# Attention and MLP in one kernel: first loads on two queues, warming products, a later weight pair, new step strings for two units, and half of q's turn behind a sum

## The chip, the cores and the metric

The kernel runs on one core of a Trainium2 chip. Times are device microseconds (us) of one execution, from start to end. Five engines have instruction streams of their own: PE (matrix products), DVE (vector), ACT (scalar functions and copies), POOL and SP, which in this kernel issues most of the DMAs; ACT issues a few. Lower is better.

## The reference, cut to what matters

```
for t in range(S):                                   # S = 768, per batch (4) and head (8), D = 48
    state = f[t][:, None] * state + outer(k[t], v[t])    # f = sigmoid(f_logit)
    y[t] = q[t] @ state
x = y, laid out as (4*768 tokens, 8*48 = 384)
h = x @ w_in                                         # w_in 384 x 2048
g = h * sigmoid(1.702 * h)
out = g @ w_out                                      # w_out 2048 x 384
```

## The kernel before, in words

**Tiling.** The 3072 tokens are cut into 12 units of 256. A unit goes through attention and then through the MLP. Attention works in chunks of 64 tokens with six levels (1, 2, 4, ... 32): at each level PE computes scores `sc` (L445), DVE multiplies the queries and keys by the running decay (L539 in units 0 and 1, L543 later), ACT copies keys aside (`Kc`, L514; later units also queries, `Qc`, L520) and masked scores go into a tile `A` (DVE L486 and L505; level 32 by ACT, L495). Then PE adds `A` times v into `y` (L555), forms the chunk sums `pd` (L666) from turned keys `kn` (L619, later units L641), DVE chains the states `st` (L691, L692), and PE adds query times state into `y` (L713). ACT copies `y` to `yT` (L728) and five or six DMAs lay it out as `xT` (L778, L783), the input of the MLP. For unit 0 ACT first reads one element of the finished sum (L677), so that PE's L713 stands behind L555.

**Turning the inputs.** f, q and k arrive in a tile `raw`. In units 0 and 1 PE turns them by a product with the identity (`t`, L376) and ACT moves the result out (L381). From unit 2 on DVE turns them by 32x32 transposes, two instructions for each input (L364), and POOL and ACT finish f (L391, L394).

**Weights.** They come as 64-bit numbers, in 16 pairs of row blocks, numbered 0 to 15 here: 576 KB for a pair of w_in, 768 KB for one of w_out. A pair is fetched on SP (L207) into one of three `bits` buffers, and turned into float32 by one ACT instruction (L239, the Prelu) and three of DVE (`a` L235, `s` L228, the sum L238). The fetch of a pair waits until the pair three before it has been read out of its buffer.

**MLP.** Units 0 and 1 use plain products (h L1127, gelu on ACT L1131, o L1141, running sum L1191 and L1193). Unit 3 and later use 20 products of quarter blocks for h (L1033), whose results DVE adds up (L1061) and ACT turns to g (L1052, L1063), and 7 products for o (L894).

**What sets the order.** PE's and POOL's order is that of the program text. In the opening and in units 1 and 2 ACT, DVE and SP follow the text too. The text of the opening is written out by hand (from L1311 on). After it, unit 1 and unit 2 of attention are emitted part by part, and after each part a string of steps (PLAN, L1363) says what is put in: `f` is the next MLP step (three h products or one o product), `c` the next step of converting a weight pair, `p` starts the conversion of the next pair (its ACT instruction), `w` fetches the next pair, `s` does a prepared sum of weights, `k` is an idle product that keeps the array at work. HOLES (L263) puts such steps inside unit 2's levels, and FIRST (L1362) ahead of unit 1. From unit 4 on a planner (`merge`, L1254) places MLP steps by their columns. In the opening `keep_up` (L110) issues idle products on `A`, which is cleared by a DVE memset (L121), ahead of the first loads.

**The places that the change touches.** `load_raw` (L269) deals a unit's four head pairs over the queues that it is given; the first pair of q in unit 0 takes three DMAs, because it begins one token early. The opening calls `load_raw` for f on SP alone, for k on SP, for q on ACT alone, then fetches weight pair 0 (L1316 to L1319). Late in the opening it starts weight pair 1 (L1351), ahead of the level-32 copies L495. In unit 1's strings the fetch of pair 8 stands ahead of y and xT of unit 1, and that of pair 9 behind them, next to the `p` of pair 8 (the part "pw").

Of the kernel before, what the change touches and what calls it, by code (L numbers as in the profile page):

```python
# [16 lines left out]
def view(t, offset, dims):  # L17

    a = t[:]
    return bass.AP(a.tensor, a.offset + offset, [list(a.ap[0])] + [list(d) for d in dims])  # L20
# [3 lines left out]
def kernel(  # L24
# [33 lines left out]
    nc = tc.nc  # L58
# [51 lines left out]
    def keep_up(times, columns=(NL - 1) * 64, of=None):  # L110

        if times:
            pt = bank([P, columns], f"idle_{next(serial)}")
        for _ in range(times):
            lhs, rhs = of or (ident, masks.rearrange("p l f t -> p (l f t)"))
            nc.tensor.matmul(pt, lhsT=lhs, rhs=rhs, start=True, stop=True)

    ones = const.tile([P, 1], F32, name="ones")
    nc.vector.memset(ones, 1.0)
    nc.scalar.activation(ones, ones, AF.Sigmoid)  # L120
    nc.vector.memset(A, 0.0)  # L121
    nc.vector.memset(ones, 1.0)
    serial = count()
    flat_A = A.rearrange("p c f t -> p (c f t)")
    keep_up(2, 192, (flat_A[:, :P], flat_A[:, :192]))

    R = U // 32
    RW = R * D + HS - D
# [131 lines left out]
            state["done"] += 2  # L260


    HOLES = {(N_FILL, 0): "ccp", (N_FILL, 1): "cwcc", (N_FILL, 2): "cwp", (N_FILL, 3): "cc", (N_FILL, 4): "cw"}  # L263

    def convert_in(n, l):

# [71 lines left out]
    def attention(n):  # L338
# [19 lines left out]
        def turn(j, outs, fn=None, pieces=None):  # L358

            if n >= N_FILL:  # L360
                for f in (1, 0):
                    out = outs(f)
                    at, step = (0, 1) if f else (HALF - 1, -1)
                    nc.vector.transpose(  # L364
                        view(out, at, [[HALF, NP], [step, R4], [R4 * step, 32]]),
                        by_half[:, j, f].rearrange("p a (j d) -> p (a j) d", j=R4)[:, :, :32],
                    )
                if fn:
                    fn()
                return  # L370
            for j0 in pieces or range(0, R, 4):
                pt = bank([P, 4, P], f"t_{n}_{j}_{j0}")
                for jj in range(4):
                    for h in range(2):
                        x = (j0 + jj) * D
                        nc.tensor.matmul(  # L376
                            pt[h * HS:(h + 1) * HS, jj, :], lhsT=by_pair[j][:, h, x:x + HS], rhs=ident, start=True, stop=True
                        )
                for f in (1, 0):
                    at, step = (j0, 1) if f else (HALF - 1 - j0, -1)  # L380
                    nc.scalar.activation(  # L381
                        view(outs(f), at, [[HALF, NP], [R * step, 16], [step, 4]]),
                        pt.rearrange("p j (a f i) -> p f a i j", a=NP, f=2)[:, 1 - f],
                        (AF.Tanh if n > 1 else AF.Sigmoid) if fn else AF.Copy, scale=0.5 if fn and n > 1 else 1.0,
                    )
            if fn and n > 1:
                half_up()
# [612 lines left out]
    def mlp_h20(n, g, before):  # L1000
        w = (width(n) + 1) // 2
        groups = 1 if FG * w <= 512 else 2
        wide = FG // groups
        order = WHOLE if groups == 1 else HALVES
        plan = [x for x in order if x[0] is not None]
        lane_of = {(x, group): lane for x, group, lane in plan}
        left = {}
        for x, group, _ in plan:
            for out, _ in PRODUCTS[x][3]:
                left[out, group] = left.get((out, group), 0) + 1  # L1010
        single = {key for key, times in left.items() if times == 1}
        begun, banks, shared, later = set(), {}, {}, {}
        in_y[n] = len(plan)

        def take(lane, name):
            if lane < 4:
                banks[lane] = bank([P, wide, w], f"h_{n}_{name}", lanes["h"][lane])
            else:
                tag = "y" if lane < 6 else "sc"
                if tag not in shared:  # L1020
                    shared[tag] = ps.tile([P, 2, 512], F32, tag=tag, name=f"h_{n}_{tag}")
                banks[lane] = shared[tag][:, lane % 2, :wide * w].rearrange("p (t x) -> p t x", x=w)
            return banks[lane]

        def product(x, group, lane):
            a, b, parent, parts = PRODUCTS[x]
            root = parent < 0
            ph = take(lane, f"{x}_{group}") if root else banks[lane]
            kids = [y for y in range(len(PRODUCTS)) if PRODUCTS[y][2] == x]
            goes_on = any(lane_of[y, group] == lane for y in kids)  # L1030
            for t in range(wide):
                f = group * wide + t
                nc.tensor.matmul(  # L1033
                    ph[:, t], lhsT=WA[a][:, f // 2, f % 2 * P:(f % 2 + 1) * P], rhs=E[n][b], start=(root and t == 0), stop=not goes_on,
                    skip_group_check=True,
                )
            in_y[n] -= 1
            for y in kids:
                if lane_of[y, group] != lane:
                    nc.scalar.copy(take(lane_of[y, group], f"{y}_{group}"), ph)  # L1040
            part, turned = ph, 1
            for out, sign in parts:
                key = out, group
                f = ROW[out // 2] * FG + group * wide
                to = g[f // HF][:, f % HF:f % HF + wide, out % 2 * w:(out % 2 + 1) * w]
                left[key] -= 1
                if key in single:
                    nc.scalar.activation(to, ph, AF.Gelu_apprx_sigmoid, scale=float(sign))
                    continue
                if key not in begun:  # L1050
                    begun.add(key)
                    nc.scalar.activation(to, ph, AF.Copy, scale=float(sign))  # L1052

                    part, turned = to, sign
                    continue
                if part is not ph and left[key]:

                    later[key] = part, sign * turned
                    continue
                for part, sign in ((part, sign * turned), *filter(None, [later.pop(key, None)])):  # L1060
                    nc.vector.tensor_tensor(to, to, part, ALU.add if sign > 0 else ALU.subtract)  # L1061
                if not left[key]:
                    nc.scalar.activation(to, to, AF.Gelu_apprx_sigmoid)  # L1063

        def begin():
            for half in range(2):
                g[half] = g_tile(f"g_{n}_{half}", width(n))
            free = lanes["o"]

            lanes["h"] = [free[x] for x in ((1, 2, 0, 3) if groups == 1 else (1, 2, 3, 0))]  # L1070
            lanes["o"] = [lanes["h"][x] for x in (1, 0, 3, 2)]

        def end():
            if n == NALL - 2:
                with tc.issue_after(copied["state"].ins):
                    sums_of_a(n, g)
                return
            sums_of_a(n, g)
            if width(n) > U:
                sum_last(g)  # L1080

        items = [(0, begin, 0)]
        for x in order:
            if x[0] is None:
                items += before[:4]
                del before[:4]
            else:
                items.append((wide * w, lambda x=x: product(*x), 0))
        assert not before
        return items + [(0, end, 0)]  # L1090
# [116 lines left out]
    def parts_of(n):  # L1207
# [3 lines left out]
        if n and n != N_FILL:  # L1211
            kind, scores = parts[0]
            _, ahead = units[n - 1][1][-1]
            def both():
                rest = ahead()
                scores()
                if rest:
                    rest()
            parts[0] = kind, both
# [91 lines left out]
    def opening():  # L1311
# [1 line left out]
        begin_f, begin, begin_k, begin_gates = units[0][0]  # L1313
        next_f, next_q, next_k, next_gates = units[1][0]
        level, evacuate, turn_k = units[0][2]
        load_raw(0, 0)  # L1316
        load_raw(0, 2)
        load_raw(0, 1, (nc.scalar,))
        fetch_weights()  # L1319
        begin_f()  # L1320
        begin_gates()
# [26 lines left out]
                units[0][3]()  # L1348
        chosen[:] = [2, 3, 2, 3]
        next_q()  # L1350
        begin_pair(1)  # L1351
        state["begin"] = 2
        evacuate(NL - 1)
        units[0][1][-2][1]()
        next_gates()
        for _ in range(NOP):
# [2 lines left out]

    fill = []  # L1360
    opening()
    FIRST = 'k'  # L1362
    PLAN = {  # L1363
        3: (
            "fffffffsffsf", "fsffsffsf", "f", "fsfsfsffsfsfsf", "", "ffff", "ff", "ffffffffffffffffsffsf", "fffsf",
        ),
        1: (
            "cccwcccwkkkkk", "kkkcf", "cfccwf", "fcffcwffcffcf", "ffcc", "f", "cwc", "fcc", "ffcf", "pw", "fw", "ff",
            "fffffff",
        ),  # L1370
        2: (
            "ffff", "ffffffff", "fcfcfcwffcfcfcwfffcfcfcff", "sss", "fcfcfcfffffss", "fcfcfcffffffff", "",
            "fffffffffff",
        ),
    }
    fill += mlp_blocks((0, 0)) + mlp_blocks((0, 1))
# [57 lines left out]
```

## Time and profile before

| what | us |
|---|---|
| three runs | 587.57, 588.43, 589.80 (median 588.43) |
| the profiled execution | 587.35 |
| its span | 585.4, so 1.95 lies around it |
| PE busy | 564.4 of the span |
| DVE, ACT, POOL busy | 441.0, 288.8, 142.5 |
| granted clock of PE, mean | 0.999 |

The views used are these. The page gives busy time by engine and the chain that ended last. The view of waits gives, for an engine, what it waited for, with total, number and longest in us. The timeline lists instructions: start, duration, engine, line, operation, output and inputs, form, number, and in brackets the idle time before it on its engine with what ended it; a q behind an engine's name marks the issue of a DMA. `xN` merges neighbours of one line. The trace also holds each DMA's issue and the landing of its last packet.

### The profile page before, as it was taken

How to read it: one execution, taken by the hardware profiler on the slowest of the kernel's cores; microseconds unless marked ns; L12 is line 12 of the kernel's file. 1: busy time of each engine (PE TensorE's matmuls, PEld its weight loads, DVE VectorE, ACT ScalarE, POOL GpSimd, SP SyncE). 2: the span in 40 equal slices, each digit the busy share in tenths (PEclk: the TensorE clock that was granted, in tenths of full speed). 3: DMA queues.
4: the chain of work that ended last, by engine and by line, in shares of the span. 5: the costliest groups of instructions: out<-in, count | busy, mean ns of one | idle time of the engine just before them, and what ended most of it. 6: DMA issues, size and time to landing. Idle time of an engine off the chain costs nothing.

```text
span 585.4 us, 18532 instructions
## 1 busy us (share of the span) xinstructions
PE 564.4 (96%) x7838; PEld 514.6 (88%) x7838; DVE 441.0 (75%) x697; ACT 288.8 (49%) x588; POOL 142.5 (24%) x226
## 2 busy tenths in 40 slices
PE   7899889999999999999999999999999999999997
PEld 6767667676899999999999999999999999999896
DVE  2898877986888786887796897786897786461284
ACT  4755354323543563564563564563563563652440
POOL 4020220614452602402502502502402403103000
PEclk9999999999999999999999999999999999999999
DMA  7869695833352452453542343442451211001000
GB/s 183 197 185 221 172 241 133 234 79 89 100 143 55 126 125 58 116 128 82 131 113 56 103 128 86 126 115 57 120 130 43 64 39 29 29 2 36 19 1 28
DMA packets 86771, 60.34 MB, mean 103 GB/s; under 512 B 33505, under 2 KB 78465, under 8 KB 86689
## 3 DMA queue, kind: packets, MB, share of 16 engines
q1 hardware_dynamic: 86208, 58.57, 40.0%
q8 instruction: 62, 1.02, 0.7%
q10 hardware_dynamic: 481, 0.59, 0.4%
q14 instruction: 20, 0.16, 0.1%
HBM read 45.49 MB, written 8.91 MB: 93 GB/s over the span
## 4 chain that ended last, share of the span: by engine, by line
PE 73%; DVE 10%; DMA 7%; SPq 4%; ACT 3%; issue 2%; ACTq 0%; DVEq 0%
PE h L1033 17%; PE o_Y L894 14%; PE o_Z L894 9%; PE h_y L1033 6%; PE sc L445 6%; PE o_X L894 5%; PE o_W L894 4%; DMA bits<-in_moe_w_in_dram 3%; PE h L1127 3%; PE o L1141 3%; DVE X L364 2%; PE y L713 2%; PE y L555 2%; PE sc L666 2%; DVE X L543 1%
## 5 line engine op out<-in xcount | busy, mean ns | idle before, releaser
L543 DVE TENSOR_TENSOR X<-X,tot 128x1024 f32<-128x1024 f32 x50 | 67.7, 1354 | 44.7 <-PE sc L445 38.4
L514 ACT COPY Kc<-X 128x512 f32<-128x512 f32 x72 | 48.4, 672 | 81.6 <-DVE X L543 61.2
L995 POOL TENSOR_TENSOR E<-xT 128x128 f32<-128x128 f32 (+1 forms) x36 | 16.0, 455 | 229.4 <-DMA xT<-yT 229.4
L1127 PE MATMUL h<-xT,w_in 128*128 128x256 f32 x288 | 65.9, 383 | 2.6 <-DMA xT<-yT 1.8
L1127 PEld LDWEIGHTS h<-xT,w_in 128*128 128x128 f32 x288 | 53.7, 190 | 12.3 <-issue 2.4
L1033 PE MATMUL h<-E,w_in 128*128 128x128 f32 (+1 forms) x476 | 62.8, 277 | 0.5 <-DVE g L1061 0.5
L1033 PEld LDWEIGHTS h<-E,w_in 128*128 128x128 f32 x476 | 57.4, 192 | 1.4 <-issue 0.8
L894 PE MATMUL o_Y<-T,S 128*128 128x192 f32 x320 | 57.7, 329 | 0.0
L1063 ACT ACTIVATE g<-g 128x512 f32<-128x512 f32 (+1 forms) x70 | 40.4, 590 | 27.1 <-DVE g L1061 26.8
L894 PEld LDWEIGHTS o_Y<-T,S 128*128 128x128 f32 x320 | 52.2, 190 | 0.6
L1061 DVE TENSOR_TENSOR g<-g,h 128x512 f32<-128x512 f32 (+1 forms) x58 | 36.1, 637 | 15.3 <-PE h L1033 14.4
L364 DVE STREAM_TRANSPOSE X<-raw 128x512 f32<-128x512 f32 x40 | 42.4, 1115 | 3.1 <-PE y L713 1.8
L1141 PE MATMUL o<-w_out,g 128*128 128x384 f32 x128 | 43.7, 491 | 0.1
L505 DVE COPY_PREDICATED A<-masks,sc 128x256 f32<-128x256 uint32 (+1 forms) x98 | 41.8, 505 | 0.1
L1141 PEld LDWEIGHTS o<-w_out,g 128*128 128x128 f32 x128 | 23.7, 190 | 14.9 <-ACT g L1131 0.4
L728 ACT COPY yT<-y 48x256 f32<-48x256 f32 (+1 forms) x66 | 21.1, 370 | 29.3 <-PE y L713 28.9
L391 POOL TENSOR_SCALAR F<-F 128x1024 f32<-128x1024 f32 x10 | 12.8, 1278 | 87.0 <-ACT F L394 87.0
L1052 ACT ACTIVATE g<-h 128x512 f32<-128x512 f32 (+1 forms) x52 | 28.6, 577 | 9.4 <-PE h L1033 9.0
L445 PE MATMUL sc<-X,Kc 48*64 48x64 f32 x1344 | 28.3, 220 | 3.7 <-ACT Kc L514 2.1
L445 PEld LDWEIGHTS sc<-X,Kc 48*64 48x64 f32 x1344 | 24.1, 134 | 8.0 <-ACT Kc L514 4.4
L894 PE MATMUL o_X<-w_out,g 128*128 128x192 f32 x160 | 29.6, 331 | 0.5 <-ACT o_X L858 0.5
L894 PE MATMUL o_W<-T,g 128*128 128x192 f32 x160 | 29.5, 331 | 0.0
(161 smaller groups left out, 1187.2 us busy)
## 6 DMA issues: line engine op xcount, KB each, us to landing
bits<-in_moe_w_out_dram SPq DMA_DIRECT2D x8, 768.0 KB
raw<-in_f_logit_dram SPq DMA_DIRECT2D x48, 96.0 KB
raw<-in_k_dram SPq DMA_DIRECT2D x48, 96.0 KB
bits<-in_moe_w_in_dram SPq DMA_DIRECT2D x8, 576.0 KB
raw<-in_q_dram SPq DMA_DIRECT2D x44, 96.0 KB
k_tok<-z SPq DMA_DIRECT2D x64, 64.0 KB
kt<-k_tok SPq DMA_DIRECT2D x16, 256.0 KB
out_dram<-osb SPq DMA_DIRECT2D x20, 192.0 KB
```

What stands on the lines that cost most here:

```text
L364: nc.vector.transpose(view(out, at, [[HALF, NP], [step, R4], [R4 * step, 32]]), by_half[:, j, f].rearrange("p a (j d) -> p (a j) d", j=R4) ...
L445: nc.tensor.matmul(t["sc"][h][g * HS:(g + 1) * HS, a, s, :], lhsT=t["Kc", l][rows(h), x:x + HS], rhs=rhs(h, a, g), start=True, stop=True,)
L505: moved = nc.vector.copy_predicated(out=view(A, c * HALF + at, dims), mask=mask.bitcast(U32), data=got)
L514: nc.scalar.copy(c.rearrange("p (n two m) -> p n two m", two=2, m=m), view(X, KF * SLOT, [[2 * m, SLOT // (2 * m)], [(KR - KF) * SLOT + m, ...
L543: nc.vector.tensor_tensor(x, x, y, ALU.mult)
L894: nc.tensor.matmul(t[name], lhsT=lhs(f), rhs=rhs(f), start=(new and i == 0), stop=(i == HF - 1), skip_group_check=True,)
L1033: nc.tensor.matmul(ph[:, t], lhsT=WA[a][:, f // 2, f % 2 * P:(f % 2 + 1) * P], rhs=E[n][b], start=(root and t == 0), stop=not goes_on, ski ...
L1052: nc.scalar.activation(to, ph, AF.Copy, scale=float(sign))
L1061: nc.vector.tensor_tensor(to, to, part, ALU.add if sign > 0 else ALU.subtract)
L1063: nc.scalar.activation(to, to, AF.Gelu_apprx_sigmoid)
L1127: nc.tensor.matmul(ph, lhsT=w_in[:, ff // 2, c, ff % 2 * P:(ff % 2 + 1) * P], rhs=xTs[n][:, c, :], start=(c == 0), stop=(c == NK - 1))
L1141: nc.tensor.matmul(t["po"], lhsT=g[ff // FG][:, ff % FG, tt * P:(tt + 1) * P], rhs=w_out[:, ff, :], start=(ff == ffs[0]), stop=(ff == ffs[ ...
```

## The change

1. **Opening loads.** The memset of `A` is split, the first 128x256 of it by itself; the number of idle products on it goes from two calls to four (two instructions each). The sigmoid that makes ACT load its table, and the memset after it, stand behind the loads. Unit 0's f is dealt over SP and ACT; of q, the first head pair stays on ACT and the other three go to SP, behind k.
2. **Weight pair 1** is no longer started in the opening. FIRST is now `p`, so its ACT instruction stands behind L677, ahead of unit 0's `yT` copies. SECOND is empty and does nothing.
3. **Step strings.** HOLES and the strings of units 1 and 2 are laid anew. In unit 1 there are three `k` fewer, counting FIRST (six idle PE instructions). Pair 5 is fetched behind unit 2's f. In unit 1 the eighth and ninth strings are now "wc" and "wffcfp": pair 9 is fetched right behind pair 8, both ahead of xT of unit 1 on SP, and the ACT instruction of pair 8 stands ahead of the `yT` copies of unit 1 on ACT (before, behind them). Between y of unit 1 and the first h of unit 1 there are six o steps, as before.
4. **q's turn.** For even units the second of q's two transposes is issued behind the last sum L1061 that was emitted. It acts in units 6, 8 and 10, which are turned while units 5, 7 and 9 run. Behind it on DVE stands the first decay product L543, and behind that on ACT `Kc` of level 2 and the second half of `kn` (L641).

```diff
     nc.vector.memset(ones, 1.0)
-    nc.scalar.activation(ones, ones, AF.Sigmoid)
-    nc.vector.memset(A, 0.0)
-    nc.vector.memset(ones, 1.0)
+    nc.vector.memset(A[:, :2], 0.0)
+    nc.vector.memset(A[:, 2:], 0.0)
...
-    keep_up(2, 192, (flat_A[:, :P], flat_A[:, :192]))
+    keep_up(4, 192, (flat_A[:, :P], flat_A[:, :192]))
...
-    HOLES = {(N_FILL, 0): "ccp", (N_FILL, 1): "cwcc", (N_FILL, 2): "cwp", (N_FILL, 3): "cc", (N_FILL, 4): "cw"}
+    HOLES = {(N_FILL, 0): "pc", (N_FILL, 1): "ccfwcc", (N_FILL, 2): "cw", (N_FILL, 3): "cc", (N_FILL, 4): "pcw"}
...
+                        if j == 1 and f == 0 and n % 2 == 0 and "sum" in copied:
+                            order.enter_context(tc.issue_after(copied["sum"].ins))
...
-                    nc.vector.tensor_tensor(to, to, part, ALU.add if sign > 0 else ALU.subtract)
+                    copied["sum"] = nc.vector.tensor_tensor(to, to, part, ALU.add if sign > 0 else ALU.subtract)
...
-        load_raw(0, 0)
+        load_raw(0, 0, (nc.sync, nc.scalar))
         load_raw(0, 2)
-        load_raw(0, 1, (nc.scalar,))
+        load_raw(0, 1, (nc.scalar, nc.sync, nc.sync, nc.sync))
+        nc.scalar.activation(ones, ones, AF.Sigmoid)
+        nc.vector.memset(ones, 1.0)
...
-        begin_pair(1)
-        state["begin"] = 2
...
-    FIRST = 'k'
+    FIRST = 'p'
+    SECOND = ''
...
         1: (
-            "cccwcccwkkkkk", "kkkcf", "cfccwf", "fcffcwffcffcf", "ffcc", "f", "cwc", "fcc", "ffcf", "pw", "fw", "ff",
-            "fffffff",
+            "ccccwcckkkkk", "ckcfwf", "fcf", "fwccfcccwfffff", "ffcf", "", "cfccc", "wc", "wffcfp", "f", "fw", "f",
+            "ffffff",
         ),
         2: (
-            "ffff", "ffffffff", "fcfcfcwffcfcfcwfffcfcfcff", "sss", "fcfcfcfffffss", "fcfcfcffffffff", "",
-            "fffffffffff",
+            "ffffff", "fffffffffc", "ccffffcfcwfcwffcfccfff", "sfs", "fsfcccffffffssf", "fcccffffffff", "",
+            "ffffffffff",
         ),
```

More of the change, by code (lines that the diff above doesn't have):

```diff
@@ L363, in turn @@
                     at, step = (0, 1) if f else (HALF - 1, -1)
[L364 to L367, printed above, removed]
+                    with ExitStack() as order:
+                        if j == 1 and f == 0 and n % 2 == 0 and "sum" in copied:
+                            order.enter_context(tc.issue_after(copied["sum"].ins))
+                        nc.vector.transpose(
+                            view(out, at, [[HALF, NP], [step, R4], [R4 * step, 32]]),
+                            by_half[:, j, f].rearrange("p a (j d) -> p (a j) d", j=R4)[:, :, :32],
+                        )
                 if fn:
@@ L1215, in both @@
                 rest = ahead()
+                if n == 1:
+                    follow_steps(SECOND)
                 scores()
```

## The prediction

> **What bounds the kernel now.** I read the page first: busy time by engine, then the chain that ended last.
>
> ```profile
> PE 564.4 (96%) x7838; PEld 514.6 (88%) x7838; DVE 441.0 (75%) x697; ACT 288.8 (49%) x588; POOL 142.5 (24%) x226
> ...
> PE 73%; DVE 10%; DMA 7%; SPq 4%; ACT 3%; issue 2%; ACTq 0%; DVEq 0%
> ```
>
> PE is busy for 564.4 of 585.4 us, so 21 us are idle. No PE work goes but a few idle products, so the change can only move those 21 us and the slow start of the array. PE's waits say what they are made of (total, number, longest):
>
> ```profile
> PE h_y L1033 <- DVE g L1061: 2.5, 3, 0.9
> PE sc L445 <- ACT Kc L514: 2.1, 2, 1.2
> PE idle L116 <- DVE A L121: 2.0, 1, 2.0
> PE h L1127 <- DMA xT<-yT: 1.8, 1, 1.8
> PE t L376 <- DMA raw<-in_f_logit_dram: 1.1, 1, 1.1
> ```
>
> Each is a place that the change touches. I take them in order of time, with the timeline of each stretch.
>
> **The opening.** Timeline from 0 to 8 us:
>
> ```profile
> 1.05 0.91 DVE L121 MEMSET A<- 128x1024 f32 x1 [0.19 <-issue]
> 2.02 1.65 PE L116 MATMUL idle<-A 128*128 128x192 f32 x4 [2.02 <-DVE A L121]
> 4.72 3.54 PE L376 MATMUL t<-ident,raw 128*64 128x128 f32 x34 [1.05 <-DMA raw<-in_f_logit_dram]
> ```
>
> A quarter of the memset is about 0.25 us, so the idle products start near 1.4. The four began 0.32 apart; eight end near 4.1. The four pieces of f landed at 2.83, 3.25, 3.72 and 4.58, with issues 0.45 apart on SP and q's between them. Dealt over SP and ACT, with no table load ahead of ACT, the last lands near 3.7. So the turn starts at 4.1, not 4.72: **-0.6**. Its products follow each other 0.107 us apart until 7.68 and 0.055 after: 29 of 96 are slow, 29 x 0.052 = 1.5 us. If warming moves the end of the slow pace as far as the start, nothing is won; if the earlier products count, nearly all 1.5. I take half, 0.7. Of q, the last piece landed at 9.46, since pair 0 (issued 5.19 and 5.60 on SP) shared the bus with ACT's pieces; now q is ahead of pair 0 on SP, and should land near 7.8. The first scores (12.64) come up to 1.7 earlier.
>
> Not all of it survives: unit 1's q lands at 22.08 in a stream that does not get shorter, and its turn starts at 22.80, so that one can move 0.7 only. Next, the weight pair that is started later (timeline 14 to 32 us):
>
> ```profile
> 26.44 0.94 ACT L239 ACTIVATE bits<-bits 128x768 f32<-128x768 f32 x1 [0.97 <-DMA bits<-in_moe_w_in_dram]
> ...
> 27.27 1.50 ACT L495 COPY A<-sc 32x256 f32<-32x256 f32 x4
> ...
> 28.96 1.10 PE L555 MATMUL y<-A,vt 64*48 64x64 f32 x62 [0.96 <-ACT A L495]
> ```
>
> PE waits 0.96 for copies that stand behind pair 1 on ACT. Without it they start when DVE's last L505 is done (26.65 less the 1.7), near 25.0, and end near 26.5. Then y waits only for PE's own t products (27.74 less 0.7) and starts near 27.0. Behind it, ACT's four evacuations (28.79 to 30.0), Kc and L677 come that much sooner. L713 began at 31.09; I get 28.5 at best, 29.8 if DVE's states keep their time. I take **-2.0** (-1.3 to -2.6) for everything up to unit 0's xT and the first h (39.12). Pair 1's instruction now stands ahead of `yT`, but its data landed at 26.36 and PE's L713 lasts longer than its 0.94: nothing. The six idle instructions that go (6 x 0.27 = 1.6) filled the wait for that xT, so they give nothing by themselves. From 38.95 to 67.57 PE runs with no gap over 0.4, so the -2.0 reaches unit 1's y.
>
> **The end of unit 1.** Timeline 60 to 78 us:
>
> ```profile
> 62.05 0.88 SPq L207 DMA_DIRECT2D bits<-in_moe_w_in_dram  x2
> 62.24 1.11 PE L713 MATMUL y<-X,st 48*48 48x64 f32 x64
> ...
> 63.47 1.96 ACT L728 COPY yT<-y 112x256 f32<-112x256 f32 x6 [2.03 <-PE y L713]
> ...
> 67.73 0.89 ACT L239 ACTIVATE bits<-bits 128x768 f32<-128x768 f32 x1 [2.29 <-DMA bits<-in_moe_w_in_dram]
> ...
> 69.36 5.55 PE L1127 MATMUL h<-xT,w_in 128*128 128x256 f32 x24 [1.78 <-DMA xT<-yT]
> ...
> 75.17 0.94 ACT L239 ACTIVATE bits<-bits 128x768 f32<-128x768 f32 x1 [4.21 <-DMA bits<-in_moe_w_in_dram]
> ...
> 76.74 0.70 PE L445 MATMUL sc<-X,Kc 48*64 48x64 f32 x32 [1.21 <-ACT Kc L514]
> ```
>
> Here I expect the loss. Pair 8 is issued at 62.05 and lands at 67.70, 5.65 later. ACT's `yT` copies started at 63.47, right behind y, and pair 8's Prelu came after them, at 67.73. Now the Prelu stands **ahead** of the copies, and they wait for pair 8. SP's stream up to pair 8 starts behind pair 0's conversion and is otherwise the same bytes, so I move it by 1.75: issue 60.3, landing 65.95, Prelu until 66.85. Queued behind it are `yT`, the DMAs of `xT`, unit 2's F, Kc and Qc. The `xT` piece that ended the wait of h was issued 3.22 after the first copy (63.47 to 66.69), and such pieces landed 1.75 to 2.53 after issue: h begins at 71.8 to 72.6. Pair 9, now ahead of xT on SP, lands some 3.15 after pair 8 (as pair 5 did after pair 4, 42.34 to 45.49), at 69.1, before that. I take 71.95: **+2.6** against 69.36, so from -2.0 the stretch loses 4.6. PE would reach it at 65.6 and stand for over 6 us, its only cover the same six o's.
>
> What comes back: pair 9 is there, so the wait of 1.21 at 76.74, behind pair 9's Prelu, goes; so, I think, does the gap of 0.59 at 82.8, since DVE has had time: **-1.8** (0 to -1.8). Next late is nothing near: from 84 to 126 PE has no gap over 0.3.
>
> A wait of 6 us has no like in the trace; the longest, 1.95 in all, left the pace as it was, while the first products ran at half pace. I bound the price by 0 and by twice the 1.5 us of the start, and take **+0.7**.
>
> [...]
>
> **q's turn**, three times; the first, 240 to 262 us:
>
> ```profile
> 243.14 2.98 DVE L364 STREAM_TRANSPOSE X<-raw 128x512 f32<-128x512 f32 x3
> ...
> 246.69 1.16 PE L1033 MATMUL h_y<-xT,w_in 128*128 128x128 f32 x8 [0.90 <-DVE g L1061]
> ```
>
> The sum PE waits for (245.97) stands behind three transposes; with one moved it comes 0.95 sooner, and the wait of 0.8 to 0.9 goes, 2.5 in all. But the moved one goes behind the sum of 255.82, and L543 (1.21), level 2's Kc (0.66) and the second kn copy (1.15) line up behind it: kn ends near 260 to 260.6, where PE would want it at 259.4 (it ended 259.92, PE took it at 260.33). So 0.6 to 1.2 comes back each time. I take **-0.5** for the three (-2.5 to +1.5).
>
> **The sum:** -2.0 at unit 1's y, +2.6 at its h, then +2.6 - 1.8 + 0.7 - 0.5 = +1.0 on 587.35, which is 588.35. The profiled execution is 1.08 under the median of the runs, so I say 589.4. About 0.5% (2.9 us) is what a measurement here can tell from no change: same is 585.5 to 591.3.
>
> **The rivals.**
> *Fast.* Pair 8 is in when unit 1's y ends, so ACT never waits. It speaks for it that the DMA engines are half idle between 56 and 63 us, against it that raw k's eight issues fill SP there. Then -2.6, -1.8 and -2.5: 581.5. It decides if pair 8 lands by 62.5 or so.
> *Late (slower).* SP's stream is no earlier, because the bus and not the opening sets it: pair 8 lands at 67.7, h begins 67.7 + 0.89 + 3.22 + 2.53 + 0.14 = 74.5, +5.1; the restart costs 1.5, only 1.2 comes back and q's turn is even: +5.4, 593.8. It decides from a landing of pair 8 past 67. The same time stands for an opening that does not do what it says.
> *Cold.* As forecast, but the array restarts at half pace for as long as the first time, from 2.02 to 7.68, half of 5.66, 2.8 instead of 0.7: 591.5.
>
> **How the numbers follow.** Forecast 0.40 (589.4, by its own terms 586.5 to 591), fast 0.24, late 0.24, cold 0.12. Same is the forecast and half of cold, 0.46; slower late and the other half, 0.30; faster 0.24. The range leaves out the outer half of fast and a little of late: 583.5 to 594.
>
> **What would show it.** Right: idle products near 1.4, t near 4.1, y L713 of unit 0 near 29; then a wait of h for xT of some 6 us at 66 to 72, ACT's L239 there waiting for bits, and no wait at the scores after it; L1061 no longer among h_y's releasers, kn at `sc` L666 instead. Wrong: pair 8 landing before y, a first h that moves by less than 1, or new waits of h and o for weights, which I cost at nothing since the conversions keep their order on DVE.

## The result and the profile after

The change makes the kernel a little slower: 591.15 us (median of 20 runs, 589.07 to 594.31) against 587.57 (20 runs, 585.28 to 589.85), a ratio of 1.0057 [1.0042, 1.0072]. That is inside the range and on the side that the sum gave (+1.0), but 3.6 us, not 1.0; the interval lies across the bound of 0.5%, so it is not clearly the "same" that I held likeliest. The profiled execution is the fastest of the 20: 589.07, with a span of 587.3, against 587.35 and 585.4. So the trace shows 1.9 us of the 3.6 only. For the rest the granted clock of the runs is a sign: its mean over after's 20 runs is 0.9922, over the runs of the kernel before in the experiments below 0.9993 to 0.9999 (a mean for each of four sets of 11 to 26 runs), and the profiled execution, at 0.994, is among the better ones of after.

The page after, busy time by engine:

```profile
PE 566.6 (96%) x7836; PEld 516.1 (88%) x7836; DVE 441.0 (75%) x698; ACT 288.9 (49%) x588; POOL 139.8 (24%) x226
```

PE has two instructions fewer and is busy 2.2 us **longer**, which points to a slower pace somewhere. PE's waits after (total, number, longest):

```profile
PE sc L668 <- ACT kn L643: 2.4, 4, 0.7
PE h L1129 <- issue: 2.0, 1, 2.0
PE h L1129 <- DMA xT<-yT: 1.9, 1, 1.9
...
PE t L378 <- issue: 1.1, 1, 1.1
```

Of the rows of before, `h_y <- g` is gone and waits for kn stand in its place, as foreseen: three of the four, 1.9 us, at 262, 350 and 438 us; the fourth, 0.48 at 171.66, lies elsewhere. The wait of 1.2 for Kc is gone too. New is "issue", twice: waits with no releaser that the profile shows. Now the places in order of time; PE's timeline, 0 to 8 us, then 24 to 41:

```profile
1.22 2.93 PE L116 MATMUL idle<-A 128*128 128x192 f32 x8 [1.22 <-DVE A L120]
4.65 3.60 PE L378 MATMUL t<-ident,raw 128*64 128x128 f32 x56 [0.51 <-DMA raw<-in_f_logit_dram]
```

```profile
27.63 0.38 PE L378 MATMUL t<-ident,raw 128*64 128x128 f32 x2 [1.14 <-issue]
...
29.78 1.04 PE L715 MATMUL y<-X,st 48*48 48x64 f32 x46 [0.71 <-ACT y L679]
...
35.92 0.81 PE L116 MATMUL idle<-masks,ident 128*128 128x320 f32 x2
38.72 2.84 PE L1129 MATMUL h<-xT,w_in 128*128 128x256 f32 x6 [1.99 <-issue]
```

The idle products start 0.8 sooner, t only 0.07: the pieces of f landed at 3.25, 3.56, 3.92 and 4.40, hardly sooner than before. But the array was warm by then: the trace's record of the full clock begins at 4.64 (7.76 before), so none of t's 96 products is at the slow pace instead of 29, and the first scores are 1.22 sooner (11.42). This profile is one of the better cases: in the eleven profiles of experiments with the same opening the full clock begins between 4.30 and 7.07 and 0 to 24 of the products come before it, and the first scores at 11.22 to 12.18; in experiment 5, with the old opening, at 9.97, with 50 products, and at 13.73. At y L715 1.31 of it is left, at the first h 0.23. Here PE first stands for 1.99 us. The timeline of 60 to 80 us, PE and ACT:

```profile
61.29 0.68 PE L668 MATMUL sc<-vt,kn 64*64 64x48 f32 x32 [0.78 <-ACT kn L621]
...
64.68 1.11 PE L715 MATMUL y<-X,st 48*48 48x64 f32 x64
...
72.26 5.81 PE L1129 MATMUL h<-xT,w_in 128*128 128x256 f32 x18 [1.93 <-DMA xT<-yT]
```

```profile
59.84 0.93 ACT L238 ACTIVATE bits<-bits 128x768 f32<-128x768 f32 x1
60.67 0.56 ACT L621 COPY kn<-tkn 128x512 f32<-128x512 f32 x1
...
65.57 0.90 ACT L238 ACTIVATE bits<-bits 128x768 f32<-128x768 f32 x1 [1.69 <-DMA bits<-in_moe_w_in_dram]
66.37 1.94 ACT L730 COPY yT<-y 112x256 f32<-112x256 f32 x6
```

y of unit 1 is 2.4 **later** than before (62.24), though the first h was sooner, and 18 products of h take 5.81 where 24 took 5.55. The second is the clock, and so are 1.7 of the first. Another 0.78 of it is a new wait: ACT's conversion of a weight pair (59.84) now stands ahead of the second kn copy (60.67), and PE's chunk sums wait for that; before, both kn copies ended at 57.25, ahead of the conversion at 57.85. The copies to `yT` begin 1.69 after y begins, where they took 1.23 before, so the Prelu of pair 8 holds them up by 0.46; the 1.69 in brackets is time in which ACT stood idle ahead of the Prelu, most of it before y was there (y ends at 65.79). The stretches from 36 to 42 and from 70 to 74 us (us, busy time of PE, PEld, DVE, ACT, POOL, then the granted clock, the DMA share and GB/s):

```profile
36.00:38.00 2.00, 0.73 (x2) 0.22 (x2) 1.87 (x3) 0.06 (x1) 0.00 (x0) 1.00 0.73 209
38.00:40.00 2.00, 1.28 (x3) 1.07 (x4) 2.00 (x5) 1.43 (x2) 0.00 (x0) 0.69 0.92 206
40.00:42.00 2.00, 2.00 (x6) 1.55 (x5) 1.51 (x4) 0.39 (x1) 0.00 (x0) 0.50 0.81 195
...
70.00:72.00 2.00, 0.33 (x2) 0.00 (x0) 2.00 (x3) 0.01 (x1) 1.82 (x2) 1.00 0.42 103
72.00:74.00 2.00, 1.74 (x6) 1.46 (x7) 0.85 (x3) 1.68 (x3) 1.76 (x4) 0.73 0.84 253
```

Behind each standstill of 2 us the clock falls to 0.50, from 38.77 to 42.19 and from 72.91 to 76.32: 3.41 us each, 1.7 us of work lost each time. Before, the same two places had a clock of 1.00 throughout.

Matching the score products of the two traces one by one gives the account in time: after stands at -1.2 at 12.6 us of before's time, at +1.45 at 58.4 (-0.23 and +1.7), at +2.4 at unit 1's y, at +2.9 at its h, at +1.9 from 135 us, and between +2.05 and +2.2 from 170 us to the end. Everything is decided in the first 170 us.

### The profile page after: what moved, and what is told of

The parts are those of the page before. It is cut to its first block, busy times and chain, and to the rows that moved or that the text cites. A ratio compares the mean times of both kernels' runs of the same rounds, so it can differ in the third digit from the quotient of the medians.

```text
span 587.3 us, 18538 instructions
## 1 busy us (share of the span) xinstructions
PE 566.6 (96%) x7836; PEld 516.1 (88%) x7836; DVE 441.0 (75%) x698; ACT 288.9 (49%) x588; POOL 139.8 (24%) x226
## 4 chain that ended last, share of the span: by engine, by line
PE 71%; DVE 11%; DMA 6%; ACT 5%; issue 3%; SPq 3%; ACTq 0%; DVEq 0%
PE h L1035 14%; PE o_Y L896 12%; PE o_Z L896 9%; PE sc L447 6%; PE h L1129 6%; PE h_y L1035 5%; PE o_X L896 5%; PE o_W L896 4%; PE y L715 2%; DVE g L1063 2%; DVE X L366 2%; PE o L1143 2%; DMA raw<-in_q_dram 2%; PE t L378 2%; PE sc L668 2%
## 5 line engine op out<-in xcount | busy, mean ns | idle before, releaser
L1129 PE MATMUL h<-xT,w_in 128*128 128x256 f32 x288 | 68.4, 396 | 4.5 <-issue 2.0
L1129 PEld LDWEIGHTS h<-xT,w_in 128*128 128x128 f32 x288 | 56.3, 198 | 15.2 <-issue 5.2
L1133 ACT ACTIVATE g<-h 128x256 f32<-128x256 f32 x48 | 17.7, 384 | 31.5 <-PE h L1129 31.2
```

The lines of the kernel that those rows point to most:

```text
L1129: nc.tensor.matmul(ph, lhsT=w_in[:, ff // 2, c, ff % 2 * P:(ff % 2 + 1) * P], rhs=xTs[n][:, c, :], start=(c == 0), stop=(c == NK - 1))
```

## The experiments

My theory after the result: the loss is the two standstills with the half clock behind them, the second made by pair 8's Prelu ahead of `yT`. The rivals: that it is the weight pairs' bytes ahead of xT; that the idle products are worth nothing and the loss lies elsewhere; that the opening itself is the loss. All ratios are to the kernel before on the same chip. Where a kernel adds or leaves out products "idle", the output is untouched.

**1. Idle products back at the first standstill** (from after):
```diff
-            "ccccwcckkkkk", "ckcfwf",
+            "ccccwcckkkkk", "ckkkkkcfwf",
```


> The changed kernel with four idle products put back (eight PE instructions, 2.15 us) in front of unit 0's first h, where PE stood still for 1.99 us. Theory (the half clock of 38.7 to 42 us is a restart after that standstill and costs 1.8): the granted clock stays at 1.00 there, the transfer of xT ends h's wait when it did (about 38.7), and the time falls by about 1.7 us, ratio to before near 1.003. Rival (the late transfers set the time, and the clock is only a by-product that later waits absorb): clock 1.00, time unchanged, ratio near 1.006.


Measured: 1.0046 [1.0029, 1.0062], 590.97. It doesn't tell the theories apart: in its profile the clock fell earlier, from 30.96 to 37.79, behind the wait marked "issue" at 29.05 (1.77 us), the ten idle products of the first string ran at that clock (4.85 us instead of 2.96), and those put back held the first h until 42.14, though xT was in at 39.09.

**2 and 3. Four idle products before unit 1's h, and both places at once:**
```diff
-            "ffffff",
+            "fffkkkkfff",
```


> The changed kernel with four idle products in front of unit 1's first h, behind the six o steps, where PE stood still for 1.93 us. Theory (restart at half clock): 72 to 76 us runs at 1.00, the time falls by about 1.8 us, ratio near 1.003. Rival: the wait for xT is all of the loss there, and the time stays, ratio near 1.006.

> Both of the two above. Theory: the two add, -3.5 us, ratio near 1.000, mean granted clock near 0.999. Rival: near 1.006; if only one of the two matters, 1.003.


Measured: 1.0132 [1.0109, 1.0155] and 1.0093 [1.0073, 1.0113]. Neither expectation came, since the products made a new wait. PE's timeline of the first, 66 to 82 us:

```profile
69.25 1.78 PE L116 MATMUL idle<-masks,ident 128*128 128x320 f32 x6
76.21 1.43 PE L116 MATMUL idle<-masks,ident 128*128 128x320 f32 x2 [5.19 <-DVE sum L1195]
77.44 4.81 PE L1129 MATMUL h<-xT,w_in 128*128 128x256 f32 x13
```

The fourth idle product turns to a bank that still holds an o, and the sum that frees it stands on DVE behind unit 2's transposes: 5.2 us. Here warming was not free, because it needed a bank.

**4. The same with the bank of the running h, six products** (from after; `K` is a new step):
```diff
+            elif step == "K":
+                chosen[:] = [int(repr(turns)[6:-1]) % 4]
+                keep_up(6)
...
-            "ffffff",
+            "fffKfff",
```


> The changed kernel with six idle products ahead of unit 1's first h, all in the bank which that h takes next, so that none waits for an evacuation. This mends the earlier run, in which the fourth product waited 5 us for DVE. Theory (restart): no half-clock window behind 70 us or a shorter one, time -1 to -1.7 us against the changed kernel, ratio 1.003 to 1.004, one window (0.003) more in the mean clock. Rival: time unchanged, 1.006.


Measured: 1.0044 [1.0028, 1.0059], 590.29. The clock stays at 1.00 around 72 us and 18 products of h take 4.15, but the twelve idle instructions hold h until 73.28. It is 0.13% under after, with overlapping intervals.

**5. Before, without any of the nine calls of idle products in its step strings:**
```diff
-    FIRST = 'k'
+    FIRST = ''
...
-            "cccwcccwkkkkk", "kkkcf",
+            "cccwcccw", "cf",
```


> The kernel before without the nine idle products of unit 1's first steps (FIRST's, and those of the first two strings), and nothing else. They stand where PE waits for Kc (35.7 to 36.6) and for unit 0's xT (37.3 to 39.1). Theory (a window of 3.41 us in which PE is busy for less than about half is followed by one at half clock): a window falls to 0.5 between 34 and 42 us, the mean clock is 0.997 or 0.994 instead of 1.00, and the time grows by 1.7 us for each that falls on the h products, ratio 1.002 to 1.005. Rival (my prediction's own: idle products fill a wait and are worth nothing): clock 1.00, ratio 1.000 within 0.001.


Measured: 1.0035 [1.0019, 1.0051], 589.45. PE's timeline, 30 to 46 us, and the granted clock:

```profile
37.87 1.13 PE L445 MATMUL sc<-X,Kc 48*64 48x64 f32 x32 [3.91 <-ACT Kc L514]
39.96 2.93 PE L1127 MATMUL h<-xT,w_in 128*128 128x256 f32 x6 [0.96 <-DMA xT<-yT]
```

```profile
40.00:42.00 2.00, 2.00 (x5) 1.63 (x6) 2.00 (x5) 1.08 (x2) 0.00 (x0) 0.50 0.95 275
```

Two windows at half clock, 37.27 to 44.10, behind a standstill of 3.9 us. All nine calls together are worth 2.1 us here; the change takes three of them away, and what those three are worth no run shows by itself.

**6. Prelu and pair 9 both behind `yT` and xT** (from after):
```diff
-            ... "wc", "wffcfp", "f", "fw", "f",
+            ... "wc", "ffcf", "pwf", "fw", "f",
```


> The changed kernel with one thing undone in unit 1's steps: pair 9's fetch and pair 8's ACT instruction stand again behind y of unit 1. Theory of the prediction (the Prelu holds yT up): yT follows y at once, h of unit 1 begins 2.5 to 2.9 us sooner with the standstill before it shorter than 1.9; the wait for pair 9 (1.2) returns behind it. Time -1.2 to -3 us, ratio 1.001 to 1.004. Rival (xT would have been late anyway, behind pair 8's transfer): h begins less than 1 us sooner, ratio 1.005 or more.


Measured: 1.0011 [0.9996, 1.0026], 588.32: 2.7 us of the loss of 3.4 are gone, and the two intervals lie apart. Its one profile does not show where. The copies to `yT` follow y as before (1.23), but h begins at 72.78, not 2.5 sooner than after's 72.26, and there are two windows at half clock as in after (from 38.44 and from 72.57). With 589.11 it is in the slower half of the 12 runs, and after's, with 589.07, is the fastest of 20.

**7. Prelu alone behind `yT`, pair 9 still ahead of xT:**
```diff
-            ... "wc", "wffcfp", "f", "fw", "f",
+            ... "wc", "wffcf", "pf", "fw", "f",
```


> The changed kernel with pair 8's ACT instruction alone moved behind unit 1's yT copies; pair 9's fetch stays ahead of xT on SP. The run that moved both came to 1.0011. Theory (the Prelu that holds yT is what costs in unit 1's steps): yT starts when y ends, the wait for xT is 3 us or less also in runs where pair 8 lands late, ratio 1.001 to 1.003. Rival (pair 9's bytes ahead of xT are what costs): xT still lands behind pair 9, the wait stays, ratio 1.005 or more.


Measured: 1.0084 [1.0065, 1.0103], 592.46. Moving the Prelu alone cures nothing. Against experiment 6 only pair 9's fetch is moved, and that is worth 0.7%, so pair 9 ahead of xT is a cause by itself. Whether the Prelu ahead of `yT` would cost anything without pair 9 is not shown: no run has the one without the other. The timelines of 60 to 80 us, first that of experiment 6, then that of 7:

```profile
65.66 1.96 ACT L730 COPY yT<-y 112x256 f32<-112x256 f32 x6 [2.03 <-PE y L715]
...
72.78 5.70 PE L1129 MATMUL h<-xT,w_in 128*128 128x256 f32 x18 [2.70 <-DMA xT<-yT]
```

```profile
64.77 1.96 ACT L730 COPY yT<-y 112x256 f32<-112x256 f32 x6 [2.03 <-PE y L715]
...
66.76 0.51 ACTq L785 DMA_DIRECT2D xT<-yT  x1
...
71.84 1.15 SPq L785 DMA_DIRECT2D xT<-yT  x2
...
75.75 4.46 PE L1129 MATMUL h<-xT,w_in 128*128 128x256 f32 x10 [6.57 <-DMA xT<-yT]
```

In 7 the copies start right behind y, yet ACT's piece of xT, issued at 66.76, lands at 71.82: pair 9 landed at 71.27. SP's next piece was issued 0.02 us after that, at 71.84. Before's trace has the same picture: ACT's piece and SP's last one carry one semaphore number there, the first landed at 68.51 and the second was issued at 68.53. So in 7 a small piece took 5.1 us, with the weight pairs' bytes issued ahead of it, and by these times it held up the pieces behind it. Part of the 5.1 may be that pair 8 is late in this profile too (landed 68.56, in after's 65.47). Even in 6 one piece waits this way (70.00, issued 70.06), and which piece shares a semaphore is not the same in every kernel (in after none of SP's pieces of this xT has the number of ACT's); no run moves that alone.

**8. After without q's turn** (`if False:` in place of its condition).


> The changed kernel with q's turn as it was before. Theory: the three waits of 0.8 to 0.9 for kn at the chunk sums of units 5, 7 and 9 go, and the three of 0.9 for the sums of g come back: time unchanged within 0.6 us, ratio near 1.006. Rival (the turn is what costs): the waits for kn go, nothing comes back, -2.4 us, ratio 1.002.


Measured: 1.0059 [1.0036, 1.0083], 590.46: q's turn is worth nothing that shows in the time. In its profile the three waits for kn (1.9 us) are gone, and of the three for the sums of g one, of 0.62, came back; from 238 to 457 us it gains 1.75 us on before, where after gains nothing. Why the median does not fall by that is open. Its profile also happens to show the end of unit 1 much as forecast:

```profile
68.15 0.92 ACT L238 ACTIVATE bits<-bits 128x768 f32<-128x768 f32 x1 [4.92 <-DMA bits<-in_moe_w_in_dram]
68.96 1.94 ACT L730 COPY yT<-y 112x256 f32<-112x256 f32 x6
...
74.86 5.52 PE L1129 MATMUL h<-xT,w_in 128*128 128x256 f32 x16 [5.20 <-DMA xT<-yT]
```

The step strings are those of after. Here pair 8 landed at 68.05, the copies to `yT` begin 4.93 after y (64.03) instead of 1.23, so the Prelu holds them up by 3.70, and two windows at half clock follow (71.74 to 78.57). After's own profile, with 0.46 and one window, is the mild picture of the same order. In the seven profiles with the Prelu ahead of `yT` (after and experiments 1 to 4, 8 and 10) the hold is 0.4 to 3.7 us; in the other seven there is none (1.23 or 1.24 from y to the copies).

**9. Before with the opening loads alone (part 1), and the same with four idle products ahead of unit 1's turn of k:**
```diff
+                chosen.insert(0, 2)
+                keep_up(4)
```


> The kernel before with the new opening loads and the four warming products alone. Theory: the first scores begin 1.2 us sooner as in the changed kernel, some 0.4 to 1.2 of it reaches unit 0's first h, the clock stays at 1.00, time -0.4 to -1.2 us, ratio 0.998 to 0.9995. Rival (the time is set at PE's 469th product, where the changed kernel waited 1.14 us for nothing that the profile names): that product begins no sooner than 28.9 us, ratio 1.000.

> The kernel before with the new opening loads and warming products, as in the run that had these alone (ratio 1.0016, clock 0.997), plus four idle products ahead of unit 1's turn of k, just before the place where PE stood still 2.2 us. Theory (PE's own instructions are what is late there: a 16 KB piece of them starts to arrive at 26.0 and PE goes on 2.5 us after that; the loss is the half-clock window behind it): the stall at product 469 shrinks or is gone, since PE reaches it later, its end stays near 28.6, the clock goes back to 1.00 and the time falls by 0.5 to 1.5 us, ratio 0.999 to 1.001. Rival (the stall is a data wait): the end of the stall moves with the products and the time stays or grows, ratio 1.002 or more.


Measured: 1.0016 [1.0003, 1.0030] and 1.0019 [1.0005, 1.0033]. The opening alone brings no time; it costs 0.9 us. In its profile PE stands 2.21 at 28.60 ("issue"), half clock follows until 32.42, and the first h is at 40.10, 1.15 later than before. With the four products that stall is gone and h is at 38.82, but in that profile xT of unit 1 is late (a wait of 4.23): its first pieces land behind pair 8 (67.52), and SP's next piece is issued as ACT's has landed (68.27, issued 68.28), as in 7 but with pair 9 not yet fetched.

**10. After with pair 1 begun in the opening, as before:**
```diff
+        begin_pair(1)
+        state["begin"] = 2
...
-    FIRST = 'p'
+    FIRST = ''
```


> The changed kernel with weight pair 1 started in the opening again, ahead of the level-32 copies. The prediction gave the later start 0.7 to 1 us of its gain. Theory now: PE's 469th product, which the changed kernel began at 27.63, begins within 0.5 us of that, because the unnamed wait there is as long as the wait for the copies was: time unchanged, ratio near 1.006. Rival (the prediction's): that product and unit 0's y come 0.7 us or more later.


Measured: 1.0088 [1.0068, 1.0108], 592.69. By the medians part 2 is a gain of about 1.8 us (0.3%), but the two intervals overlap, so it is not clearly shown. Product 469 began at 28.89 instead of 27.63; as it began anywhere from 27.63 to 29.05 in the other profiles with the new opening and the later start, this settles neither theory.

**11. Everything warm:** order of 6, the four products of 9, four more idle instructions before the first h, and four products before unit 1's h in the running bank.


> The changed kernel with pair 8's ACT instruction and pair 9's fetch behind y of unit 1, as in the run that undid them, and idle products in all three places where PE stood still long enough to be slowed: four ahead of the last turn of unit 0's stretch (PE's product 469), two more ahead of unit 0's first h, four in one bank of their own ahead of unit 1's first h. Theory (what the change loses is restarts at half clock, 1.7 us each, plus the Prelu ahead of yT): granted clock 0.999 or 1.00 in nearly all runs, time 2 to 3 us under the run without the products, ratio 0.996 to 0.999. Rival (the products only displace waits, and their banks and instructions cost): ratio 1.001 or more.


Measured: 1.0010 [0.9997, 1.0024], 588.37, with a mean granted clock of 0.9995. The clock is whole again and nothing is won on experiment 6 (0.9952): the first h is at 39.76 where it was 38.49, so the products cost what they save. None of the versions beats the kernel before.

## Why the prediction was nearly right, point by point

The number fell inside its range by luck. At unit 1's h the sum had -2.0 + 4.6 = +2.6, and +2.9 came, but as +2.4 and +0.5: the first term was off by 4.4 one way, the second by 4.1 the other.

- **Opening.** Right that the idle products start near 1.4 (1.22) and that the slow pace shrinks; t at 4.1 was wrong (4.65), since the second queue hardly hurried f (last piece at 4.40 instead of 4.58). In after's profile all 29 slow products were cured, 29 x 0.052 = 1.5, where I took half; 0.3 of it went into a wait for k, and t ends 1.21 sooner. In other profiles of the same opening it was less.
- **"I take -2.0 for everything up to the first h."** Wrong. L715 came at 29.78, my "29.8 if DVE's states keep their time" (-1.3), but the first h moved by -0.23: it falls under my own mark, "a first h that moves by less than 1". Two things were missed: PE's stall marked "issue" at its 469th product, and pair 4, now issued at 34.95 (36.26 before), whose bytes are on the way together with xT of unit 0; the last pieces of that xT landed at 38.88 and 39.24 (38.62 and 38.79 before). That pair 4 delayed them is argued from these times; no run moves it alone.
- **"They filled the wait for that xT, so they give nothing by themselves."** This is the step that failed most. As time they gave nothing; as work they kept the clock. Experiment 5 prices all eighteen instructions at 2.1 us. With six fewer, PE stood 1.99 us and ran at half clock to 42.19, 1.7 us of work. With that and the wait of 0.78 for the second kn copy, which I had put at nothing, y of unit 1 was not -2.0 but +2.4.
- **The end of unit 1.** The Prelu ahead of `yT` did stand in the way, but for 0.46 in after's profile, and 3.70 in experiment 8's; h at 71.95 was forecast and 72.26 came. The number is right by two errors: y was 4.4 later than thought and the copies were held up that much less. Pair 8 landed at 65.47 for the 65.95 forecast, 0.32 before y ended, which comes close to my mark for wrong, "pair 8 landing before y", and the wait of h for xT was 1.93, not some 6 (5.20 in experiment 8's profile). "New waits of h and o for weights" came too: o stood 0.40 for w_out at 66.19.
- **"Pair 9 ... at 69.1, before that"**, so at no cost. It landed at 69.39, and in after's profile the pieces of xT, kept back by the Prelu until 67.67, land 2.0 to 2.6 after their issue: nothing of pair 9 shows. But it is not free. Without the Prelu in front (experiment 7) a piece of xT lands at 71.82, behind pair 9 (71.27), and the time is no better; with both gone (experiment 6) 2.7 us come back. So the delay that the experiments show is the one that I put at nothing; the one that I named is seen in the traces, and its own price is open.
- **What comes back, -1.8.** Right in its parts: the waits of 1.21 and 0.59 are gone, and one of 0.82 at 127.58 that I hadn't counted, against a new one of 0.54 at 122.14.
- **The restart, +0.7 of 0 to 3.0.** That half clock would follow a wait was right, the size not: two windows of 1.7 in the profile, and over the runs, 0.9922 against some 0.9994, 0.0072 x 587 = 4.2 us of work lost. Not all of it becomes time, since in part of such a window PE stands anyway. My bound from the trace, that a wait of 1.95 left the pace as it was, held for that wait only.
- **q's turn, -0.5.** Right within what can be seen: 2.5 of `h_y` waits became 1.9 of kn waits, and the distance to before is +2.20 at 222 us and +2.19 at 449.
- **Cold (591.5)** came nearest to the median, though not as it was meant: not one restart as long as the first, but one to four windows of 1.7.

How the half clock comes is shown in part. Both stretches at half clock in after are 3.41 us long, and their starts are 34.13 apart, ten such lengths. PE did not stand still for the whole of the 3.41 us ahead of them: it was busy for 42% (1.43 of 3.41) and 44%, where a stretch of before (65.79 to 69.20) with PE busy for 52% was followed by full clock. The busy share alone does not decide between these: counted in the same lengths from each profile's changes of clock, stretches with 43% (experiment 3) and 46% (experiment 1) were followed by full clock, one with 51% (experiment 4) by half.

**Open.** The stall at product 469 is in after and in every experiment with the new opening but two, the second of 9 and 11, which put products ahead of it and so come to it later; it is 1.1 to 2.4 us long. PE goes on 2.4 to 2.8 us after a transfer of 16 KB on the queue "instruction" begins (in after 24.87 and 27.63), and another such stall lies 127 products earlier (342, experiment 5) and 128 later (597, experiment 6). In before's own profile the wait of 0.96, which the prediction laid to ACT's copies, ends at the 469th product too, 2.84 after such a transfer (26.12) and 0.20 after the last copy (28.76), though another product of the text stands at that number; so part of what part 2 was to win back may have been this stall. That PE runs out of instructions and waits for the next piece is my reading of these times, and if it holds it caps what a faster opening can bring; it is argued from positions, not shown by an experiment that changes only the count. Open too is what the Prelu ahead of `yT` costs by itself, and why experiment 6's profile does not show its gain. Why experiment 11 wins nothing on 6 with a whole clock is told by its later h only in one profile.

## What to carry to other kernels

A weight transfer that was issued ahead of small ones on the way to the next stage cost 0.7% here (experiment 7 against 6), although it landed first (71.27, ACT's piece 71.82): count its bytes, and look for a semaphore that the small pieces share (the next was issued at 71.84), before calling the place free. The dummy products that filled a wait were not waste here (nine calls, 2.1 us in experiment 5): price their removal by the clock behind the gap, not by the gap, and mind the bank that they need and the product that they delay: put back in three places they won nothing here. And before speeding up an opening, look at what stands at its end: here 1.2 us won at 12 us had shrunk to 0.2 at 39.

## What the runs showed of the hardware that I had not expected

- PE's clock fell to half behind a standstill of 1.99 us and one of 1.93 in after. It stayed full behind one of 2.3 in experiment 3, of which 1.96 fell into the stretch of 3.41 us with PE busy for 43%, and behind one of 1.84 in experiment 1.
- The half clock lasted 3.41 us both times in after, with PE busy throughout, and 6.83 in experiments 1, 5 and 8 among others. In experiment 5 (37.27 to 44.10) PE was busy for 54% of the first 3.41 of it and for all of the second.
- These stretches did not start at one time: at 38.77 in after, 38.44 in experiment 6, 38.45 in experiment 4, 37.27 in experiment 5. Nor did the runs of one kernel lose the same: after's have mean clocks from 0.997 to 0.988, which at 3.41 x 0.5 / 587 = 0.003 for each stretch is one to four of them, and spread from 589 to 594. Those with 0.988 average 592.6, those with 0.994 590.4.
- Apart from that at the first h (38.72 in after), which in experiment 4 is a wait for xT, PE's longer waits with the releaser "issue" come at products 342, 469 and 597, 127 and 128 apart (1.1, 1.1 to 2.4 and 0.4 us long), 2.4 to 2.9 us after a transfer on the instruction queue began (in after 2.76, from 24.87, and at the first h 2.90, from 35.82).
- In experiment 7 SP issued nothing for 5.2 us, from 66.61 until 0.02 after ACT's transfer had landed (71.84); in experiment 6 and the second of 9 such a stand was 1.3 and 2.5 us long, in before 1.3 (67.22 to 68.53). In before's trace the two transfers carry the same semaphore number; that this is what holds SP is argued from the numbers and the times.
